# Table rows for the upper partitions from GpSimd's queue, and four wide matmuls in place of 32 narrow ones, in an FFT, soft-MoE and feed-forward kernel

## The chip, the cores and the metric

The kernel runs on one core of a Trainium2 chip. The metric is device time in microseconds of one execution. Three runs of the kernel before took 1397.17, 1400.21 and 1401.28 us: a median of 1400.21, a spread of 4.1 us or 0.3%. One more execution was profiled, and all rows below are from that one.

## The reference

```python
X = np.fft.fft(x, axis=1); X = np.fft.fft(X, axis=2)     # x (8, 3072, 256)
x = X.real.reshape(B * S, D)                             # 24576 tokens of 256
logits = x @ phi                                         # 32 slots
d = softmax(logits, axis=0)                              # over all tokens
slot_input = d.T @ x                                     # 8 experts x 4 slots
slot_out[e] = np.maximum(slot_input[e] @ w1[e], 0) @ w2[e]
c = softmax(logits, axis=1)                              # over the slots
y = c @ slot_out
g = s * np.maximum(y @ w_in, 0) ** 2 + b                 # 256 to 2048
out = g @ w_out                                          # 2048 to 256
```

The transformed tokens are never written out. The logits need only x projected by the transform of phi, transformed along the sequence, and the sums for the slots work likewise on the other side. The sequence of 3072 is split as 24 by 128, so that a transform along it is one matrix product over 128, a set of small tables with the twiddle factors, and one over 24.

## The kernel before, in words

The first 251 us prepare the slots, in stages. Then comes the main loop over blocks of 384 tokens, to the end.

*Pages to T (0 to about 90 us).* The sync queue (SP) loads x in 24 pages of 1 MB (xb). For each of the eight batches `emit_v` projects three pages by phd (tile vt, L394, in two parts per batch), `turn_v` turns the result on TensorE (vq, L415) and copies it to v, and `emit_t` multiplies v by the transform matrix f_sb. The result is T, in PSUM; ScalarE or VectorE copies it to SBUF as tile tt, 32 partitions at a time. The last batch is different. The first half of its T (tpa, L428) is four matmuls of 128 columns, copied by ScalarE in eight copies (L432). The second half (tpb, L439) is 32 matmuls with 32 columns of weights and 64 moving columns; they place their results so that VectorE copies them in two copies (L445).

*Order of the loads.* The sync queue issues in the order of a string, `ORDER`: x pages, four quarters of w_out (raw, "w"), two tables for the logits ("l", ltab, in two pages of 32 positions each), two tables for the sums ("h", htab), and the first pages of x for the sums ("r", xrt). The last x page is followed by one xrt page, the ltab loads (L363), the htab loads (L352) and more xrt pages.

*Tables.* An ltab page has 128 partitions, of which the upper 64 hold the same numbers as the lower 64. Before, the sync queue loads the lower 64 in two transfers of 32 rows, and GpSimd copies them to the upper 64 (L512, L513). An htab page has 112 rows: 0 to 47 and 64 to 111 are the same 48 rows of the table, loaded by two transfers of the sync queue, with zeros from GpSimd between (L350) and in alternate columns (L357).

*Logits (about 90 to 106 us).* 16 groups of eight matmuls (lp, L570) multiply tt by ltab, half of them from partitions 0 to 63 and half from 64 to 127, into six buffers of PSUM. ScalarE copies each group (lg, L583), and VectorE takes its maximum for each slot (cm, L585). After the last one the maximum over all tokens is formed; it is needed before any exponential.

*H, sums, experts, main loop.* H (112 to 145 us): exponentials (dt), 128 matmuls with htab (hp, L652), copies (hh, L643). Sums (145 to 204): products with the second pass over x (racc, L727). Experts (204 to 251). Main loop: y, hidden layer and output for all tokens (L1121, L1151, L1154).

Beside these, VectorE and GpSimd turn w_out from 64-bit to 32-bit floats in the first stage: VectorE's steps on raw and wo (L154 to L174, maximum L222, rests L216), GpSimd's sums into bias (L276), ScalarE's casts (L212).

Instructions on each engine run in the order in which the code is written; a planner's running times (`at`) decide only which engine takes a copy and when the side work on w_out is put in. The change leaves those numbers as they are.

Of the kernel before, what the change touches and what calls it, by code (L numbers as in the profile page):

```python
# [8 lines left out]
F32 = mybir.dt.float32  # L9
# [23 lines left out]
def tile_fft2__then__softmoe__then__act_relu2(  # L33
# [18 lines left out]
    nc = tc.nc  # L52
    P = 128
# [4 lines left out]
    M = 2 * NS1  # L58
# [8 lines left out]
    NR = 32  # L67
# [15 lines left out]
    f_sb = early.tile([P, P], F32, name="f_sb")  # L83
# [259 lines left out]
    tt = tpool.tile([P, 64, NG, NE], F32, name="tt")  # L343
    ltabs, htabs = [], []

    def htab_load(i):

        t, k = page([R, 16, 2, 4 * MH], F32, "htab_t")
        htabs.append((t, k))
        nc.gpsimd.memset(t[32:64], 0.0)  # L350
        for q in range(2):
            nc.sync.dma_start(out=t[64 * q:64 * q + M], in_=htab[:, 32 * i:32 * i + 32].rearrange("r (k q) m -> r k q m", q=2))  # L352
        dma_ready(2.5)

    def htab_clear(i):
# [3 lines left out]
    def ltab_load(i):  # L359
        t, k = page([P, 32, P // 2], F32, "ltab")  # L360
        ltabs.append((t, k))
        for c in range(2):
            nc.sync.dma_start(out=t[NR * c:NR * c + NR], in_=ltab[64 * c:64 * c + M, 32 * i:32 * i + 32].rearrange(  # L363
                "(j g) q m -> g j q m", j=2)[0:NR // 2])
        dma_ready(2.57)

    with tc.tile_pool(name="xtp", bufs=1, side="right") as xtp, tc.tile_pool(name="vp", bufs=1, side="right") as vp, \
            tc.tile_pool(name="ps_v", bufs=1, space=PSUM) as psv:
        mxp[:] = [psv, 4]
        vs = [vp.tile([P, NG, NE, NR], F32, name=f"v{k}") for k in range(2)]  # L370
# [52 lines left out]
        def emit_t(b):  # L423
            bg, bq = divmod(b, NG)
            if b == B - 1:
                t = psv.tile([P, 4, P], F32, tag="vq", name="tpa", bufs=2)
                for k in range(4):
                    nc.tensor.matmul(t[:, k, :], lhsT=vs[bg][:, bq, 4 * k:4 * k + 4, :].rearrange("p j n -> p (j n)"),  # L428
                                     rhs=f_sb, start=True, stop=True)
                for j in range(4):  # L430
                    for c in range(2):
                        nc.scalar.copy(tt[64 * bg + NR * c:64 * bg + NR * c + NR, :, bq, 8 * j:8 * j + 4],  # L432
                                       t[NR * j:NR * j + NR, :, 64 * c:64 * c + 64].rearrange("p e k -> p k e"))
                t = psv.tile([P, 2, 4, 64], F32, tag="vt", name="tpb", bufs=2)
                for k in range(4, 8):
                    for j in range(4):
                        for c in range(2):
                            q = 64 * (j // 2) + NR * c
                            nc.tensor.matmul(t[q:q + NR, j % 2, k - 4, :], lhsT=vs[bg][:, bq, 4 * k + j, :],  # L439
                                             rhs=f_sb[:, 64 * c:64 * c + 64], start=True, stop=True,  # L440
                                             tile_position=(0, q), skip_group_check=True)
                for eh in range(2):
                    src = t[64 * eh:64 * eh + 64].rearrange("p j k m -> p m j k")
                    dst = tt[64 * bg:64 * bg + 64, :, bq, 16 * eh:16 * eh + 16].rearrange("p m (j k) -> p m j k", j=2)
                    nc.vector.tensor_copy(dst[:, :, :, 4:8], src)  # L445
                at["pe"] += 3.0
                return
            t = psv.tile([P, 8, P], F32, tag="tps", name="tps", bufs=2)
            for k in range(8):
                nc.tensor.matmul(t[:, k, :], lhsT=vs[bg][:, bq, 4 * k:4 * k + 4, :].rearrange("p j n -> p (j n)"),  # L450
                                 rhs=f_sb, start=True, stop=True)
            at["pe"] += 2.0
            waiting = any(side_at[w[0]] < at["pe"] + 4 for w in side_work)
            eng = "act" if waiting or b >= B - 4 or at["act"] < at["dve"] + 1 else "dve"
            for j in range(4):
                for c in range(2):
                    busy(eng, 0.7 if eng == "dve" else 0.6)
                    r = 64 * bg + NR * c
                    args = (tt[r:r + NR, :, bq, 8 * j:8 * j + 8],
                            t[NR * j:NR * j + NR, :, 64 * c:64 * c + 64].rearrange("p e k -> p k e"))  # L460
                    if b == B - 2:
                        late_t.append(lambda args=args: nc.scalar.copy(*args))
                    else:
                        (nc.scalar.copy if eng == "act" else nc.vector.tensor_copy)(*args)  # L464
# [44 lines left out]
            f()  # L509
        for n in range(2 * B - 2, 2 * B):  # L510
            turn_v(n)
        nc.gpsimd.tensor_copy(ltabs[0][0][64:P], ltabs[0][0][0:64])  # L512
        nc.gpsimd.tensor_copy(ltabs[1][0][64:P], ltabs[1][0][0:64])  # L513
        for _ in range(4):
            side_step(0.0, True)
        emit_t(B - 1)
# [41 lines left out]
    with tc.tile_pool(name="ps_l", bufs=6, space=PSUM) as psl, \  # L558
# [3 lines left out]
        for st in range(NCH // 2 + SKEW):  # L562
            halves = [(h, st - SKEW * h) for h in range(2) if 0 <= st - SKEW * h < NCH // 2]
            lps = {h: psl.tile([R, KC, NG * NE], F32, name="lp") for h, _ in halves}
            for k in range(2 * KC):
                q = P // 2 * (k % 2)
                m = M if q else P // 2
                for h, i8 in halves:
                    r = slice(64 * h, 64 * h + 64)
                    nc.tensor.matmul(  # L570
                        lps[h][q:q + m, k // 2, :], lhsT=ltabs[i8 // 4][0][r, 2 * KC * (i8 % 4) + k, 0:m],
                        rhs=tt[r, 2 * KC * i8 + k].rearrange("p b e -> p (b e)"), start=True, stop=True,
# [737 lines left out]
```

## Time and profile before

| | |
|---|---|
| three timed runs | 1397.17, 1400.21, 1401.28 us |
| span of the profiled execution | 1411.6 us |
| TensorE matmul passes (PE) | 1388.2 us busy, 98%, x9036 |
| VectorE (DVE) | 1171.9 us busy, 83% |
| ScalarE (ACT) | 1010.7 us busy, 72% |
| GpSimd (POOL) | 233.1 us busy, 17% |
| DMA | 112.27 MB, mean 80 GB/s |

The span is 11.4 us longer than the median of the runs. One fp32 matmul of the code shows as two passes. PE are matmul passes and PEld weight loads; they overlap.

The rows below have these columns. A row of the busy time by stages: the stretch in us, its length, then for PE, PEld, DVE, ACT and POOL the busy time with the number of instructions, then the clock granted to TensorE (1.00 is full speed), the busy share of the 16 DMA engines, and GB/s. A row of a timeline: start and length in us, engine, line, operation, output and inputs, shapes, number of instructions, and in brackets the idle time before it and what ended that. A row of the groups by line: the line, engine, operation, shapes and count, then busy us and mean ns of one, then the idle time just before.

### The profile page before, as it was taken

The numbers are of one execution on the slowest core, as the hardware profiler recorded it, in microseconds if no ns is written. First come the engines' busy times: TensorE is split into PE (matmuls) and PEld (weight loads), VectorE is DVE, ScalarE is ACT, GpSimd is POOL, SyncE is SP. The second block draws the span as 40 slices with busy tenths as digits, with TensorE's granted clock in tenths as the row PEclk, the third lists the DMA queues.
The fourth block names the chain that finished last, engine by engine and source line by source line (L and its number), as shares of the span: only waits on it lengthen the run. The fifth ranks groups of instructions, "written<-read, shape, count | busy, mean of one in ns | idle before, by whom it ended". The sixth has DMA issues, their size and how long they took to land.

```text
span 1411.6 us, 23102 instructions
## 1 busy us (share of the span) xinstructions
PE 1388.2 (98%) x9036; PEld 856.0 (61%) x9036; DVE 1171.9 (83%) x1490; ACT 1010.7 (72%) x1423; POOL 233.1 (17%) x287
## 2 busy tenths in 40 slices
PE   8989999999999999999999999999999999999998
PEld 5669564566666666666666666666666666666665
DVE  1565764998989999999989898989898989888886
ACT  2774314877777777777877787877777777777775
POOL 1143400021212121211112121111111111111110
PEclk9995999999999999999999999999999999999999
DMA  8995795101010101101010101010101010101001
GB/s 352 414 311 229 291 414 225 29 27 36 20 36 23 36 24 29 30 23 32 23 36 21 34 23 36 23 33 23 36 23 36 23 36 23 33 23 36 23 20 30
DMA packets 72381, 112.27 MB, mean 80 GB/s; under 512 B 33904, under 2 KB 59632, under 8 KB 64976
## 3 DMA queue, kind: packets, MB, share of 16 engines
q1 hardware_dynamic: 72144, 110.70, 23.1%
q8 instruction: 71, 1.16, 0.3%
q14 instruction: 38, 0.31, 0.1%
q0 software_dynamic: 128, 0.10, 0.0%
HBM read 78.48 MB, written 25.17 MB: 73 GB/s over the span
## 4 chain that ended last, share of the span: by engine, by line
PE 88%; DMA 2%; DVE 1%; issue 1%; SPq 0%; ACT 0%; POOL 0%; DVEq 0%; ACTq 0%; POOLq 0%
PE op L1151 46%; PE op L1154 23%; PE fhp L1121 12%; PE racc L727 3%; DMA w2t<-in_moe_w_dram 2%; PE hp L652 2%; PE dps L712 1%; PE lp L570 1%; SPq L1084 0%; DVE cm L585 0%; DVE r L1127 0%; DVE rhl L1112 0%; PE eop L957 0%; DMA g<-gs 0%; PE gp L1055 0%
## 5 line engine op out<-in xcount | busy, mean ns | idle before, releaser
L1151 PE MATMUL op<-whl,rhl 128*128 128x512 f16 x3072 | 1025.3, 379 | 0.8 <-ACT rhl L1111 0.6
L1154 PE MATMUL op<-whl,rhl 128*128 128x256 f16 x3072 | 835.7, 273 | 0.0
L1126 ACT ACTIVATE r<-fhp,wsc 128x768 f32<-128x768 f32 (+1 forms) x513 | 461.8, 900 | 230.0 <-PE fhp L1121 228.8
L1127 DVE SCALAR_TENSOR_TENSOR r<-fhp,r 128x768 f32<-128x768 f32 (+1 forms) x513 | 488.9, 953 | 113.6 <-ACT r L1126 104.0
L1112 DVE TENSOR_TENSOR rhl<-r,rhl 128x768 f16<-128x768 f32 x511 | 506.9, 992 | 0.9 <-ACT rhl L1111 0.9
L1151 PEld LDWEIGHTS <-rhl 128*128 128x128 f16 x3072 | 300.5, 98 | 335.4 <-ACT rhl L1111 0.9
L1111 ACT CAST rhl<-r 128x768 f16<-128x768 f32 x511 | 420.1, 822 | 1.8 <-DVE r L1127 1.8
L1154 PEld LDWEIGHTS <-rhl 128*128 128x128 f16 x3072 | 300.6, 98 | 62.7 <-issue 0.3
L1166 POOL TENSOR_TENSOR ot<-ot,bias 128x256 f32<-128x256 f32 x189 | 138.1, 731 | 974.2 <-DVE ot L1164 974.2
L1121 PE MATMUL fhp<-ct,g 128*128 128x384 f16 x1024 | 250.4, 326 | 1.1 <-DMA g<-gs 0.8
L1121 PEld LDWEIGHTS <-g 128*128 128x128 f16 x1024 | 99.9, 98 | 69.0 <-issue 1.1
L1163 ACT ACTIVATE o<-op,small 128x256 f32<-128x256 f32 x189 | 90.0, 477 | 16.7 <-PE op L1154 16.7
L1164 DVE SCALAR_TENSOR_TENSOR ot<-op,small,o 128x256 f32<-128x256 f32 x192 | 91.7, 478 | 0.3
L394 PE MATMUL vt<-xb,phd 128*64 128x384 f32 (+3 forms) x288 | 49.0, 477 | 5.3 <-DMA xb<-in_x_turned_dram 5.3
L727 PE MATMUL racc<-xrt,dh 128*64 128x256 f32 x384 | 44.5, 383 | 0.4 <-DVE dh L717 0.4
L394 PEld LDWEIGHTS vt<-xb,phd 128*64 128x64 f32 x288 | 26.5, 139 | 25.5 <-issue 13.8
L727 PEld LDWEIGHTS racc<-xrt,dh 128*64 128x64 f32 x384 | 26.3, 137 | 20.9 <-issue 4.5
L419 DVE COPY v<-vq 128x512 f32<-128x512 f32 (+1 forms) x15 | 8.3, 593 | 33.9 <-PE vq L415 33.9
L406 ACT COPY vts<-vt 128x512 f32<-128x512 f32 (+1 forms) x16 | 8.5, 533 | 32.1 <-PE vt L394 32.0
L464 ACT COPY tt<-tps 32x512 f32<-32x512 f32 x48 | 27.7, 577 | 4.9 <-PE tps L450 4.4
L652 PE MATMUL hp<-htab_t,dt 112*128 112x104 f32 x128 | 27.6, 422 | 0.2 <-ACT dt L669 0.2
L652 PEld LDWEIGHTS hp<-htab_t,dt 112*128 112x128 f32 x128 | 27.4, 333 | 0.5 <-issue 0.5
(229 smaller groups left out, 518.0 us busy)
## 6 DMA issues: line engine op xcount, KB each, us to landing
xb<-in_x_turned_dram SPq DMA_DIRECT2D x24, 1024.0 KB, 20.1
xrt<-in_x_pages_dram SPq DMA_DIRECT2D x24, 1024.0 KB, 13.9
out_dram<-ot SPq DMA_DIRECT2D x128, 128.0 KB, 1.7
w1t<-in_moe_w_dram SPq DMA_DIRECT2D x8, 1024.0 KB, 13.7
out_dram<-ot SPq DMA_DIRECT2D x128, 64.0 KB, 2.0
raw<-in_moe_w_out_dram SPq DMA_DIRECT2D x4, 1024.0 KB, 20.3
raw<-in_moe_w_in_dram SPq DMA_DIRECT2D x4, 1024.0 KB, 7.8
w2t<-in_moe_w_dram SPq DMA_DIRECT2D x4, 1024.0 KB, 17.8
```

Of the source, the lines that this page charges most:

```text
L652: nc.tensor.matmul(hp[q][:, k, :], start=True, stop=True, lhsT=dt.rearrange("p k g e -> p (k g e)")[:, 128 * (2 * k + q):128 * (2 * k + q) ...
L727: nc.tensor.matmul(raccs[acc][64 * h:64 * h + 64, :], lhsT=dh[:, m, g].rearrange("p j e -> p (j e)"), rhs=xr[k][0][:, g, t, :], start=(sum ...
L1111: nc.scalar.copy(a, r2)
L1112: nc.vector.tensor_tensor(out=l, in0=r2, in1=a, op=ALU.subtract)
L1121: nc.tensor.matmul(hp[k * split][:, k, :].rearrange("p (s b m) -> p s b m", s=2, b=B), lhsT=g16[:, f * P:(f + 1) * P], rhs=c, start=True, ...
L1126: nc.scalar.activation(out=r[:, k], in_=hp[i][:, k], func=AF.Relu, scale=wsc[:, 2, p:p + 1])
L1127: nc.vector.scalar_tensor_tensor(out=r2[:, k], in0=hp[i][:, k], scalar=0.0, in1=r[:, k], op0=ALU.max, op1=ALU.mult)
L1151: nc.tensor.matmul(op.rearrange("p h d -> p (h d)"), lhsT=a, rhs=w.rearrange("p h d -> p (h d)"), start=(f == 0), stop=False)
L1154: nc.tensor.matmul(op[:, 0, :], lhsT=l, rhs=w[:, 0, :], start=False, stop=(f == NFC - 1))
L1163: nc.scalar.activation(out=o1, in_=op[:, 1, :], func=AF.Copy, scale=qv)
L1164: nc.vector.scalar_tensor_tensor(out=ot, in0=op[:, 0, :], scalar=qv, in1=o1, op0=ALU.mult, op1=ALU.add)
L1166: nc.gpsimd.tensor_tensor(out=ot, in0=ot, in1=bias, op=ALU.add)
```

## The change

Tables: `ltab_load` issues four transfers per page in place of two, of 32 rows and 256 KB each. The two for the lower partitions stay on the sync queue, the two for the upper are issued by GpSimd; GpSimd's two copies on the chip go. Of the two htab transfers of a page the one for partitions 64 to 111 moves from the sync queue to GpSimd. T: the second half of the last batch is made like the first half, by four matmuls of 128 columns, and eight copies of 32 partitions on VectorE.

```diff
@@ htab_load @@
         for q in range(2):
-            nc.sync.dma_start(out=t[64 * q:64 * q + M], in_=htab[...])
+            (nc.gpsimd if q else nc.sync).dma_start(out=t[64 * q:64 * q + M], in_=htab[...])
@@ ltab_load @@
         for c in range(2):
-            nc.sync.dma_start(out=t[NR * c:NR * c + NR], in_=ltab[...])
+            for h in range(2):
+                r = 64 * h + NR * c
+                (nc.gpsimd if h else nc.sync).dma_start(out=t[r:r + NR], in_=ltab[...])
@@ emit_t, last batch @@
-                t = psv.tile([P, 2, 4, 64], F32, tag="vt", name="tpb", bufs=2)
+                t = psv.tile([P, 4, P], F32, tag="vt", name="tpb", bufs=2)
                 for k in range(4, 8):
-                    for j in range(4):
-                        for c in range(2):
-                            q = 64 * (j // 2) + NR * c
-                            nc.tensor.matmul(t[q:q + NR, j % 2, k - 4, :], lhsT=vs[bg][:, bq, 4 * k + j, :],
-                                             rhs=f_sb[:, 64 * c:64 * c + 64], start=True, stop=True, ...)
-                for eh in range(2):
-                    src = t[64 * eh:64 * eh + 64].rearrange("p j k m -> p m j k")
-                    dst = tt[64 * bg:64 * bg + 64, :, bq, 16 * eh:16 * eh + 16].rearrange(...)
-                    nc.vector.tensor_copy(dst[:, :, :, 4:8], src)
+                    nc.tensor.matmul(t[:, k - 4, :], lhsT=vs[bg][:, bq, 4 * k:4 * k + 4, :].rearrange("p j n -> p (j n)"),
+                                     rhs=f_sb, start=True, stop=True)
+                for j in range(4):
+                    for c in range(2):
+                        nc.vector.tensor_copy(tt[64 * bg + NR * c:64 * bg + NR * c + NR, :, bq, 8 * j + 4:8 * j + 8],
+                                              t[NR * j:NR * j + NR, :, 64 * c:64 * c + 64].rearrange("p e k -> p k e"))
@@ after turn_v of the last batch @@
-        nc.gpsimd.tensor_copy(ltabs[0][0][64:P], ltabs[0][0][0:64])
-        nc.gpsimd.tensor_copy(ltabs[1][0][64:P], ltabs[1][0][0:64])
```

GpSimd's instructions before, from the memset for the first htab page (htab_t_571) on; bias_76 are the sums of w_out, of which wo_398 is the second half, and ltab_547 and ltab_550 are the two logits tables:

```order
L350 MEMSET htab_t_571 32x1664
L276 TENSOR_TENSOR bias_76<-bias_76,wo_398 128x256 x4
L350 MEMSET htab_t_612 32x1664
L512 COPY ltab_547<-ltab_547 64x2048
L513 COPY ltab_550<-ltab_550 64x2048
L276 TENSOR_TENSOR bias_76<-bias_76,wo_398 128x256 x4
```

The same place now, with the second logits table as ltab_552 and the htab pages as htab_t_575 and htab_t_616:

```order
L365 DMA ltab_547<-in_ltab_dram 32x1x2048 x2
L365 DMA ltab_552<-in_ltab_dram 32x1x2048 x2
L350 MEMSET htab_t_575 32x1664
L352 DMA htab_t_575<-in_htab_dram 48x1664
L276 TENSOR_TENSOR bias_76<-bias_76,wo_398 128x256 x4
L350 MEMSET htab_t_616 32x1664
L352 DMA htab_t_616<-in_htab_dram 48x1664
L276 TENSOR_TENSOR bias_76<-bias_76,wo_398 128x256 x4
```

The four ltab transfers stand ahead of the first memset, where GpSimd had nothing; the second htab transfer stands behind the first sums of wo_398; the two copies behind the second memset are gone.

TensorE's instructions before, from the end of the last batch's projection (vt) over its turning (vq) and T (tpa, tpb) to the first logits (lp); v_113 is the second half of the v tiles:

```order
L394 MATMUL vt<-xb,phd 64x256
L394 MATMUL vt<-xb,phd 64x128
L415 MATMUL vq<-ident,vts 128x128 x7
L428 MATMUL tpa<-f_sb,v_113 128x128 x4
L439 MATMUL tpb<-f_sb,v_113 32x64 x32
L190 MATMUL warm<-ones 128x128 x4
L570 MATMUL lp<-tt,ltab 64x128
```

The same place now:

```order
L396 MATMUL vt<-xb,phd 64x256
L396 MATMUL vt<-xb,phd 64x128
L417 MATMUL vq<-ident,vts 128x128 x7
L430 MATMUL tpa<-f_sb,v_113 128x128 x4
L438 MATMUL tpb<-f_sb,v_113 128x128 x4
L190 MATMUL warm<-ones 128x128 x4
L566 MATMUL lp<-tt,ltab 64x128
```

Nothing is reordered: 32 narrow matmuls have become four wide ones, 28 fewer, between the first half of T and the four matmuls on ones that precede the logits.

VectorE's instructions before, from the last steps on w_out's fourth quarter (wo, wsc) to the maxima of the logits:

```order
L174 SCALAR_TENSOR_TENSOR wo<-raw,wo 128x1024
L222 TENSOR_REDUCE wsc<-wo 128x2
L204 TENSOR_SCALAR wsc<-wsc 128x2
L205 RECIPROCAL wsc<-wsc 128x2
L445 COPY tt<-tpb 64x64x2x4 x2
L585 TENSOR_REDUCE cm<-lp 112x32 x13
```

And now:

```order
L174 SCALAR_TENSOR_TENSOR wo<-raw,wo 128x1024
L222 TENSOR_REDUCE wsc<-wo 128x2
L204 TENSOR_SCALAR wsc<-wsc 128x2
L205 RECIPROCAL wsc<-wsc 128x2
L442 COPY tt<-tpb 32x64x4 x8
L581 TENSOR_REDUCE cm<-lp 112x32 x13
```

The copies stand where they stood, eight of 32 partitions in place of two of 64.

## Rows read from the trace of the kernel before

**Rows 1.** Busy time by stages: the H stage and the main loop

```profile
112.00:145.00 33.00, 32.78 (x151) 31.66 (x151) 14.27 (x26) 16.44 (x34) 12.19 (x10) 0.51 0.46 182
...
251.00:1411.00 1160.00, 1156.18 (x7113) 695.92 (x7113) 1038.38 (x1276) 902.39 (x1224) 179.46 (x223) 1.00 0.11 29
```

**Rows 2.** Sync queue's timeline and its transfers: the last x page

```profile
60.43 1.73 SPq L289 DMA_DIRECT2D xb<-in_x_turned_dram  x1
...
xb<-in_x_turned_dram SPq DMA_DIRECT2D x1, 1024.0 KB, 20.5
```

**Rows 3.** TensorE's timeline, 66 to 84 us: parts of the projection

```profile
68.07 4.97 PE L394 MATMUL vt<-xb,phd 128*64 128x384 f32 x32 [0.42 <-DMA xb<-in_x_turned_dram]
...
81.28 2.38 PE L394 MATMUL vt<-xb,phd 128*64 128x384 f32 x20
```

**Rows 4.** VectorE's timeline, 84 to 104 us

```profile
88.19 1.39 DVE L445 COPY tt<-tpb 64x512 f32<-64x512 f32 x2
92.20 4.50 DVE L585 TENSOR_REDUCE cm<-lp 112x32 f32<-112x512 f32 x7 [2.61 <-ACT lg L583]
100.98 1.29 DVE L585 TENSOR_REDUCE cm<-lp 112x32 f32<-112x512 f32 x2 [4.28 <-ACT lg L583]
102.69 1.29 DVE L585 TENSOR_REDUCE cm<-lp 112x32 f32<-112x512 f32 x2 [0.42 <-ACT lg L583]
```

**Rows 5.** Chain that ended last, 84 to 112 us: start, us, what

```profile
95.01 3.88 issue
98.89 4.80 PE lp L570 x86
```

**Rows 6.** DMA queues: whole span, 78.6 to 96.3, 96.3 to 97.6 us

```profile
q8 instruction: 71, 1.16, 0.3%
...
q14 instruction: 1, 0.01, 0.1%
...
q8 instruction: 1, 0.02, 5.6%
```

**Rows 7.** Busy time in 78.6 to 95.1 us

```profile
78.60:95.10 16.50, 14.08 (x251) 11.01 (x248) 11.34 (x17) 14.98 (x31) 4.76 (x4) 1.00 1.03 214
```

**Rows 8.** GpSimd's timeline, 50 to 96 us

```profile
54.90 3.15 POOL L276 TENSOR_TENSOR bias<-bias,wo 128x256 f32<-128x256 f32 x4 [15.45 <-DVE wo L174]
63.59 1.48 POOL L350 MEMSET htab_t<- 32x1664 f32 x1 [5.54 <-PE vt L394]
...
89.32 1.89 POOL L512 COPY ltab<-ltab 64x2048 f32<-64x2048 f32 x1 [12.06 <-DMA ltab<-in_ltab_dram]
```

**Rows 9.** Busy time while x alone moves, and while the tables move

```profile
20.00:58.00 38.00, 36.99 (x258) 24.91 (x254) 19.03 (x27) 21.60 (x40) 5.05 (x7) 1.00 1.02 415
86.00:92.00 6.00, 4.48 (x123) 4.08 (x125) 3.44 (x6) 5.83 (x14) 1.89 (x1) 1.00 1.03 183
```

**Rows 10.** TensorE's timeline, 84 to 104 us: the matmuls before the pause

```profile
94.36 0.65 PE L570 MATMUL lp<-tt,ltab 64*64 64x128 f32 x10 [0.17 <-DVE cm L585]
```

**Rows 11.** Groups by line and shape, 86 to 90 us

```profile
L439 PE MATMUL tpb<-f_sb,v 128*32 128x64 f32 x64 | 1.1, 221 | 0.0
```

**Rows 12.** Groups by line and shape, VectorE, 145 to 205 us

```profile
L717 DVE COPY dh<-dps 128x256 f32<-128x256 f32 x2 | 0.8, 424 | 0.6 <-PE dps L712 0.6
```

**Rows 13.** ScalarE's timeline, 84 to 104 us

```profile
87.22 2.98 ACT L432 COPY tt<-tpa 32x256 f32<-32x256 f32 x8
90.22 1.33 ACT L212 ACTIVATE whl<-wo,wsc 128x512 f16<-128x512 f32 x2
```

**Rows 14.** Groups by line and shape, 112 to 145 us

```profile
L652 PE MATMUL hp<-htab_t,dt 112*128 112x104 f32 x128 | 27.6, 422 | 0.2 <-ACT dt L669 0.2
...
L669 ACT ACTIVATE dt<-dt 112x512 f32<-112x512 f32 x15 | 9.3, 627 | 0.4 <-POOL dt L633 0.4
...
L643 ACT COPY hh<-hp 128x208 f32<-128x208 f32 x16 | 8.2, 514 | 13.5 <-PE hp L652 13.5
```

More of the change, by code (lines that the diff above doesn't have):

```diff
@@ L351, in htab_load @@
         for q in range(2):
-            nc.sync.dma_start(out=t[64 * q:64 * q + M], in_=htab[:, 32 * i:32 * i + 32].rearrange("r (k q) m -> r k q m", q=2))
+            (nc.gpsimd if q else nc.sync).dma_start(out=t[64 * q:64 * q + M], in_=htab[:, 32 * i:32 * i + 32].rearrange("r (k q) m -> r k q m", q=2))
         dma_ready(2.5)
@@ L362, in ltab_load @@
         for c in range(2):
-            nc.sync.dma_start(out=t[NR * c:NR * c + NR], in_=ltab[64 * c:64 * c + M, 32 * i:32 * i + 32].rearrange(
-                "(j g) q m -> g j q m", j=2)[0:NR // 2])
+            for h in range(2):
+                r = 64 * h + NR * c
+                (nc.gpsimd if h else nc.sync).dma_start(
+                    out=t[r:r + NR], in_=ltab[64 * c:64 * c + M, 32 * i:32 * i + 32].rearrange("(j g) q m -> g j q m", j=2)[0:NR // 2])
         dma_ready(2.57)
@@ L433, in emit_t @@
                                        t[NR * j:NR * j + NR, :, 64 * c:64 * c + 64].rearrange("p e k -> p k e"))
-                t = psv.tile([P, 2, 4, 64], F32, tag="vt", name="tpb", bufs=2)
+                t = psv.tile([P, 4, P], F32, tag="vt", name="tpb", bufs=2)
                 for k in range(4, 8):
-                    for j in range(4):
-                        for c in range(2):
-                            q = 64 * (j // 2) + NR * c
-                            nc.tensor.matmul(t[q:q + NR, j % 2, k - 4, :], lhsT=vs[bg][:, bq, 4 * k + j, :],
-                                             rhs=f_sb[:, 64 * c:64 * c + 64], start=True, stop=True,
-                                             tile_position=(0, q), skip_group_check=True)
-                for eh in range(2):
-                    src = t[64 * eh:64 * eh + 64].rearrange("p j k m -> p m j k")
-                    dst = tt[64 * bg:64 * bg + 64, :, bq, 16 * eh:16 * eh + 16].rearrange("p m (j k) -> p m j k", j=2)
-                    nc.vector.tensor_copy(dst[:, :, :, 4:8], src)
+                    nc.tensor.matmul(t[:, k - 4, :], lhsT=vs[bg][:, bq, 4 * k:4 * k + 4, :].rearrange("p j n -> p (j n)"),
[4 more added lines that the diff above has]
+                                              t[NR * j:NR * j + NR, :, 64 * c:64 * c + 64].rearrange("p e k -> p k e"))
                 at["pe"] += 3.0
```

## The prediction

> **What bounds the kernel now.** I read the busy time by stages first, then the chain of waits, then the rows of the stretch that the change touches. The last 1,160 us (from 251 to 1411) are TensorE at its full clock, busy for 1156.2 of them [rows 1]; nothing in the change reaches that loop. What the change touches lies between 58 and 112 us, and from there on every stage waits for the one before: the pages for the sums (145 to 204) come free as TensorE uses them. So a microsecond won or lost before 112 us comes out at the end as about one microsecond, and I cost only that stretch.
>
> The stretch has two bounds in turn. Up to 83 us it is the stream of x pages. The sync queue keeps its transfers about 20 us ahead: the last x page was issued at 60.43 and landed 20.5 us later, at 80.9 [rows 2]; TensorE began the work that needs it at 81.28, one stage earlier it stood 0.42 us for a page, and otherwise it runs without a gap [rows 3]. Transfers and TensorE are level, with 0.4 us to spare: whatever holds the last pages up holds TensorE up.
>
> From 90 us it is the logits stage: TensorE fills PSUM (L570), ScalarE copies, VectorE takes the maxima, about 0.64 us each (seven in 4.50) [rows 4]. Its chain has one odd piece: from 95.01 TensorE stands 3.88 us with "issue", waiting for nothing that the profile shows, and then runs 4.80 us [rows 5]. VectorE finishes its backlog and then idles 4.28 us; with the short wait behind it (0.42) and another like it some 5.0 us go [rows 4]. I read this as TensorE waiting for its own instructions. Its 18,072 matmul passes and weight loads (9036 each) come in 71 packets of the instruction queue q8 [rows 6], about 255 to a packet. Between 78.6 and 95.1 TensorE uses 251 + 248 = 499 of them [rows 7], two packets' worth, and up to 96.3 no q8 packet lands (the one instruction packet of that time is q14's); the next of q8 falls into 96.3 to 97.6 [rows 6], and TensorE goes on 1.3 us later. The DMA engines are full then, with the tables.
>
> **The change, part by part.**
>
> Upper table rows from GpSimd's queue. Four transfers of 256 KB (1.05 MB) are new: the upper halves of ltab were copied on chip before. Two of 312 KB move from the sync queue. The order shows where: GpSimd issues the ltab rows before its first memset for htab. In the trace GpSimd is done with its sums at 54.90 + 3.15 = 58.05 and stands 5.54 us idle until that memset [rows 8]; the new issues wait for data long landed and for a VectorE step near 60 us, so they leave at 58 to 61 us. That is beside the x pages still in flight, not behind them as the sync queue's own ltab rows are. htab's first 0.32 MB follows the memset, still ahead of the last x pages; its second comes after VectorE's work on w_out, too late to hold x up.
>
> What 1.37 MB cost the x stream has two bounds. At the rate of loads into all 128 partitions, 415 GB/s [rows 9], 3.3 us. At the rate when the tables alone are moving, into 32 or 48 partitions, 183 GB/s [rows 9], 7.5 us. I take the value nearer to the second: all the new rows go into the upper 64 partitions, so I give them half of 415, 207 GB/s, while the other half goes on with x: 6.6 us. Less the 0.4 us to spare: +6.2 us on the start of everything after x. The floor below would be 0, if GpSimd's transfers only used gaps; the DMA share over 20 to 58 us is 1.02 [rows 9], so there are none, but I keep it as a rival.
>
> [...]
>
> What goes: GpSimd's two copies, the first from 89.32 on, 1.89 us [rows 8], the second as long behind it. From its start to the pause TensorE stood 0.17 us, and for VectorE [rows 10]; worth 0.
>
> T's last half. TensorE: 64 passes of 0.22 us in 1.1 us go [rows 11], eight like those of the first half in about the same time come; worth 0. VectorE: two copies of 64x512 in 1.39 us [rows 4] become eight of 32x256. A copy of 128x256 out of PSUM takes 0.424 us [rows 12]; eight make 3.39. From the same start (88.19) they end at 91.58 and not 89.58. ScalarE's own eight copies end at 87.22 + 2.98 = 90.20 [rows 13], which was what the logits stage waited for; now it waits for VectorE, 1.38 us more. But ScalarE casts weights until 90.22 + 1.33 = 91.55 before its first copy of logits [rows 13]. The matmuls ahead of the pause, about one group of logits, take 0.65 us [rows 10]: begun at 91.58 they are done at 92.23, so that copy starts 0.65 us later and no more: +0.65 us. Bounds 0.2 (0.36 us a copy, as on ScalarE) and 1.4. Queued behind the eight copies on VectorE is only the first maximum, which waits for that same copy.
>
> The pause. The order shows 28 fewer matmuls just before the logits, each two passes and two weight loads: 112 instructions fewer. So the packet that TensorE lacked is needed 28 matmuls later in the logits, at the 90th instead of the 62nd of 128. By then VectorE has about five groups of logits in hand, some 3 us of cover (5 x 0.64). But the packet is also asked for later, inside the logits. With the fetch taking as long behind x and table traffic as it does now, I get a pause of about 3 us of which 1 shows: 4 of the 5.0 us come back. Two bounds: all 5.0 come back, or none, if the fetch falls worse.
>
> Here the profiled execution has to be set against the timed runs. Its span is 1411.6 us, the median of the runs 1400.2, 11.4 us less. The last 1,160 us have no such slack, so the timed runs are shorter in the first 251 us, and the pause may be one of the things that they don't have; then nothing comes back. I take half of the 4 us: -2.0.
>
> Sum: +6.2 + 0.65 - 2.0 = +4.85 us. Against the profiled span that is 1416.4; against the median of the runs 1405.0, which I predict.
>
> **Rivals.**
>
> 1. The x stream is held up by the smaller bound alone (3.3 - 0.4 = 2.9): 2.9 + 0.65 - 2.0 = +1.55, 1401.8. For it: 16 engines share the packets. Against: the table rows of [rows 9] at half the rate.
> 2. x is late by the full 6.2, but the pause is in the timed runs and goes whole: 6.2 + 0.65 - 5.0 = +1.85, 1402.1. For it: three runs within 4 us of each other, so the pause is there always or never.
> 3. Faster: GpSimd's transfers don't hold up x, as a queue whose packets are served after the sync queue's, and the pause goes: 0.65 - 5.0 = -4.35, 1395.9. It decides where x is late by less than 0.15 us (0.15 + 0.65 - 5.0 = -4.2). Against: no gap in the DMA share before 80 us.
> [...]
> 5. The pause stays as long as it is or grows, with the x delay of the larger bound (7.1): 7.1 + 0.65 = +7.75, 1408.0.
>
> [...]
>
> **How the numbers follow.** My forecast 0.42, rival 1 0.22, rival 2 0.13, rival 3 0.10, rival 4 0.04, rival 5 0.09. A measurement of this kernel can tell from no change about 0.3%, 4.2 us: slower is above 1404.4, faster below 1396.0. Slower: 0.42 + 0.09 = 0.51. Rivals 1 and 2 are no change, 0.35, with 0.01 of rival 3's near edge 0.36. Faster: 0.10 + 0.04 less that edge, 0.13. The range holds forecast, rivals 1 and 2, and rival 5 with the larger bound (7.1 + 1.4 + 0.5 = 9.0, 1409.2), and reaches towards rival 3 without all of it: 1396.5 to 1409.5. The forecast's own range is 1403 to 1408.
>
> **What would show it.** The x step: the last three x pages land 3 to 7 us later than 20 us after their issue and TensorE stands as long for them before the last quarter of v; wrong, if they land as before. The copies: VectorE's eight end after ScalarE's eight, and the first logits matmul waits for VectorE. The pause: a stretch of "issue" on TensorE inside the logits, at about the 90th matmul, with VectorE idle about 1 us; if it is as long as before and VectorE idle 4 us, the term is wrong. The copies on GpSimd are gone and nothing has moved for them. The whole is wrong if the logits stage begins no later than now, or if the time changes behind 251 us.

## The result, and the profile after

The changed kernel takes 1411.77 us (median of 4 runs, 1410.15 to 1414.52) where the kernel before took 1400.74 (4 runs): a ratio of 1.0089, 95% interval 1.0074 to 1.0104. It is slower by about 11 us. The forecast was +4.85, with a range that ended at 1409.5: the sign was right, the size less than half.

The span of its profiled execution is 1412.7 us, 1.1 more than that of before. That comparison misleads, and the first experiment shows why: in some executions of several of these kernels TensorE runs the H stage at a lower granted clock (0.50 for its matmuls in before, 1.00 in the changed kernel), they take 27.6 us and not 14.5, and the whole takes some 13 us more, as in the profiled executions of before, ltab_only and late_rows and, by their times, in 3 of the 86 timed runs of before and in 4 of the 12 of t_only, the most of any kernel beside late_rows (2 of 6).

TensorE's timeline of the changed kernel (start, us, engine, line, operation, shapes, count; in brackets the idle time before it and what ended that), against [rows 3]:

```profile
78.11 7.39 PE L396 MATMUL vt<-xb,phd 128*64 128x384 f32 x32 [9.95 <-DMA xb<-in_x_turned_dram]
...
95.95 3.84 PE L396 MATMUL vt<-xb,phd 128*64 128x384 f32 x20 [2.15 <-DMA xb<-in_x_turned_dram]
...
108.43 11.73 PE L566 MATMUL lp<-tt,ltab 64*64 64x128 f32 x256 [3.75 <-ACT whl L212]
```

TensorE stands for x twice, 12.1 us in all, where it stood 0.42. The sync queue's timeline and its transfers say the same of the last x page, against [rows 2]:

```profile
60.85 5.53 SPq L289 DMA_DIRECT2D xb<-in_x_turned_dram  x1
...
xb<-in_x_turned_dram SPq DMA_DIRECT2D x1, 1024.0 KB, 35.0
```

It was issued at nearly the same time as before (60.85 us, then 60.43), and took 35.0 us in place of 20.5. The chain that ended last (start, us, what) has it as one piece:

```profile
60.85 34.97 DMA xb<-in_x_turned_dram
```

GpSimd's timeline shows what was put beside it, against [rows 8]:

```profile
56.12 3.14 POOL L276 TENSOR_TENSOR bias<-bias,wo 128x256 f32<-128x256 f32 x4 [14.68 <-DVE wo L174]
59.20 1.03 POOL L365 DMA_DIRECT2D ltab<-in_ltab_dram  x2
61.46 0.98 POOL L365 DMA_DIRECT2D ltab<-in_ltab_dram  x2 [1.23 <-DVE whl L216]
64.05 1.48 POOL L350 MEMSET htab_t<- 32x1664 f32 x1 [1.62 <-PE vt L396]
65.48 0.50 POOL L352 DMA_DIRECT2D htab_t<-in_htab_dram  x1
```

The busy time by stretches (the last three numbers: TensorE's clock, the busy share of the DMA engines, GB/s), against [rows 9]:

```profile
20.00:58.00 38.00, 38.00 (x263) 26.88 (x260) 18.91 (x26) 20.91 (x38) 3.89 (x6) 0.98 1.02 415
63.00:77.00 14.00, 5.16 (x39) 3.57 (x35) 5.66 (x7) 6.49 (x12) 1.93 (x2) 0.85 1.03 237
87.00:91.00 4.00, 4.00 (x27) 2.56 (x26) 2.95 (x5) 3.74 (x7) 0.00 (x0) 1.00 1.04 250
```

While GpSimd's rows are in flight (63 to 77, and 87 to 91 for the second htab page) the DMA engines are as busy as before, but x and tables together move at 237 and 250 GB/s, not at 415.

After each stand TensorE's matmuls are slower: the 32 passes at 78.11 take 7.39 us where they took 4.97, and the 20 at 95.95 take 3.84 where they took 2.38 [rows 3]. The clock granted from 95.95 to 99.73 us was 0.60 on average, 1.00 at first and 0.50 from 96.75 us on:

```profile
95.95:99.73 3.78, 3.77 (x21) 2.40 (x21) 0.00 (x0) 0.00 (x0) 0.00 (x0) 0.60 1.07 171
```

The copies of T and what follows, VectorE's timeline first, then ScalarE's, against [rows 4, 13]:

```profile
104.75 3.47 DVE L442 COPY tt<-tpb 32x256 f32<-32x256 f32 x8
```

```profile
103.35 2.98 ACT L434 COPY tt<-tpa 32x256 f32<-32x256 f32 x8
106.35 1.33 ACT L212 ACTIVATE whl<-wo,wsc 128x512 f16<-128x512 f32 x2
110.47 0.58 ACT L579 COPY lg<-lp 112x512 f32<-112x512 f32 x1 [2.78 <-PE lp L566]
```

VectorE's eight copies take 3.47 us and end at 108.22, 1.9 us after ScalarE's (106.33), and TensorE's logits begin at 108.43: it waits for VectorE, though the row names a cast of ScalarE that had been done for 0.7 us. (In wide_t below, which has the same copies, the row of the same wait names VectorE's.) The logits then run 11.73 us without a pause.

### The profile page after: what moved, and what is told of

Same layout as the page of the kernel before. It is cut to its first block, busy times and chain, and to the rows that moved or that the text cites. A ratio compares the mean times of both kernels' runs of the same rounds, so it can differ in the third digit from the quotient of the medians.

```text
span 1412.7 us, 23014 instructions
## 1 busy us (share of the span) xinstructions
PE 1377.3 (97%) x8980; PEld 844.6 (60%) x8980; DVE 1173.5 (83%) x1496; ACT 1009.2 (71%) x1423; POOL 232.1 (16%) x291
## 4 chain that ended last, share of the span: by engine, by line
PE 91%; DMA 6%; DVE 2%; SPq 1%; ACT 1%; issue 0%; DVEq 0%; ACTq 0%
PE op L1147 46%; PE op L1150 23%; PE fhp L1117 12%; DMA xb<-in_x_turned_dram 3%; PE racc L723 3%; PE vt L396 3%; DMA w2t<-in_moe_w_dram 2%; PE hp L648 1%; PE dps L708 1%; DVE cm L581 1%; PE tps L448 1%; SPq L1080 0%; PE lp L566 0%; PE vq L417 0%; DVE r L1123 0%
## 5 line engine op out<-in xcount | busy, mean ns | idle before, releaser
L396 PE MATMUL vt<-xb,phd 128*64 128x512 f32 (+3 forms) x288 | 54.0, 519 | 16.0 <-DMA xb<-in_x_turned_dram 16.0
L396 PEld LDWEIGHTS vt<-xb,phd 128*64 128x64 f32 x288 | 30.7, 151 | 36.4 <-issue 19.6
L462 ACT COPY tt<-tps 32x512 f32<-32x512 f32 x48 | 27.6, 576 | 5.1 <-PE tps L448 4.6
L770 POOL TENSOR_TENSOR lg<-lg,rm 112x512 f32<-112x512 f32 x16 | 22.4, 1404 | 4.2 <-DVE rm L768 4.2
L752 POOL TENSOR_TENSOR lg<-et,lg 112x512 f16<-112x512 f32 x16 | 18.5, 1156 | 0.0
## 6 DMA issues: line engine op xcount, KB each, us to landing
w1t<-in_moe_w_dram SPq DMA_DIRECT2D x8, 1024.0 KB, 13.3
```

The source lines that it names most:

```text
L396: nc.tensor.matmul(vt[64 * h:64 * h + 64, o:o + k, :], lhsT=phd[:, c, sg, :], rhs=turned(pg, c, i, k, rev), start=(c == 0 and m < 2), stop ...
```

## Experiments

Each of these kernels was timed against the kernel before, 6 or 12 times; only b_again, extra_upper and extra_even were run once, for their profiles. Diffs are against the kernel before. In the expectations "theory A" and "theory B" are two explanations that the run is to tell apart.

**b_again: the kernel before, once more.** No edit.

> The kernel before, unchanged, profiled once more. In its first profile the 128 hp matmuls of the H stage took 27.61 us at half clock and the span was 1411.6 us, 11 us above the timed runs; in the profile of the changed kernel they took 14.51 at full clock. Theory A (the half clock of that stage belonged to that one profiled execution): hp takes about 14.5 us here, the span is about 1411.6 - 13.1 = 1398.5, and the pause on TensorE in the logits is there or not independently of it. Theory B (the half clock is part of every execution of the kernel before, and the profiler costs 11 us elsewhere): hp takes 27.6 us again, span 1411 to 1412.

Measured: span 1399.4 us. The groups by line of before ([rows 14]: 27.6 us) have here

```profile
L652 PE MATMUL hp<-htab_t,dt 112*128 112x104 f32 x128 | 14.6, 276 | 0.2 <-DMA xrt<-in_x_pages_dram 0.2
```

and TensorE's timeline has the pause, in two parts (the last part of x, the first logits, the pause, and the beginning of H):

```profile
82.60 2.37 PE L394 MATMUL vt<-xb,phd 128*64 128x384 f32 x20 [0.66 <-DMA xb<-in_x_turned_dram]
...
91.57 6.20 PE L570 MATMUL lp<-tt,ltab 64*64 64x128 f32 x124 [1.52 <-ACT tt L432]
100.21 2.64 PE L570 MATMUL lp<-tt,ltab 64*48 64x128 f32 x86 [2.44 <-issue]
...
106.50 0.69 PE L570 MATMUL lp<-tt,ltab 64*64 64x128 f32 x4 [1.74 <-issue]
...
114.67 14.57 PE L652 MATMUL hp<-htab_t,dt 112*128 112x104 f32 x128 [0.21 <-DMA xrt<-in_x_pages_dram]
```

Theory A. The 11.4 us between the profiled span and the runs were the H stage at the lower clock, 27.6 - 14.6 = 13.0 us (granted 0.50 from 114.5 to 142.2 us of before, 0.98 from 112 to 146 us here); the pause is in this undisturbed execution too. From here on b_again stands for the profile of before.

**t_only and tables_only: one part of the change each.**

```diff
 t_only:      32 narrow matmuls and two copies -> four wide ones and eight copies; tables as before
 tables_only: ltab_load, htab_load as in the change, GpSimd's copies gone; T as before
```

> The kernel before with the T part of the change alone: four matmuls of 128 columns, eight copies on VectorE; tables as before. Theory A (the table rows on GpSimd's queue are the whole loss): x lands as before (last page at about 80.9 us), VectorE's eight copies take 3.4 us and end 1.4 to 2 us later than the two did, the pause is shorter by 1 us or more; time within 2 us of before, 1399 to 1403. Theory B (the copies and the later start of the logits carry a good part of the loss): 1404 to 1408.

> The kernel before with the tables part of the change alone: upper ltab rows and second htab rows from GpSimd's queue; T by 32 matmuls and two copies as before. Theory A (the table rows are the whole loss, because x packets slow down beside them): last x page lands at about 95.8 us and not 80.9, TensorE stands about 9.5 us for a page and then about 2 us for the last; time 1409 to 1413. Theory B (about half of the loss is T's): 1404 to 1408.

Measured: t_only 1402.2 us, ratio 1.0036 (1.0006 to 1.0065), or 1400.0 against 1399.98 without its four longer executions (1413.6 to 1418.4). tables_only 1410.8 us, ratio 1.0086 (1.0069 to 1.0102), nearly the whole change. Theory A for both: the loss is the tables', unless T makes the longer executions more frequent, which these runs don't decide (wide_t below, with the same T, has 2 in 12, wide_tables none). In t_only TensorE's timeline shows both sides of T:

```profile
96.86 10.68 PE L566 MATMUL lp<-tt,ltab 64*64 64x128 f32 x256 [3.51 <-ACT whl L212]
```

It stands 3.51 us before the logits (1.52 in b_again), and then no pause stops it. Against theory A, x did not land as before in this execution: TensorE stood 3.16 us for the last page, with nothing new beside x. Of tables_only, TensorE's wait for the page was

```profile
77.71 7.96 PE L396 MATMUL vt<-xb,phd 128*64 128x384 f32 x32 [9.76 <-DMA xb<-in_x_turned_dram]
```

The second wait of theory A, about 2 us for the last page, is not there: that page landed at 93.1 us, not at 95.8, in an execution that was the shortest of its six (1407.3 us).

**ltab_only: the upper ltab rows alone from GpSimd.**

```diff
+            for h in range(2):
+                r = 64 * h + NR * c
+                (nc.gpsimd if h else nc.sync).dma_start(out=t[r:r + NR], in_=ltab[...])
-        nc.gpsimd.tensor_copy(...)   # both copies
```

> The kernel before with the upper ltab rows alone from GpSimd's queue as in the change (four transfers of 32 rows, 1.05 MB, at 58 to 62 us), no copies; htab on the sync queue, T as before. Theory A (the loss goes with the narrow rows in flight beside x): the x page that TensorE needs at about 68 us is late by 7 to 8 us and not 10; all of x is late by that; time +6 to +9, 1405 to 1408. Theory B (the htab rows carry the loss, being the ones still in flight when the last x pages are): +1 to +3.

Measured: 1406.85 us, ratio 1.0052 (1.0022 to 1.0083); TensorE stood 8.13 us for the page. Theory A: ltab has 7.5 us of the loss. That leaves some 3 to 4 us of tables_only's for the htab rows, by difference: they were not run alone.

**wide_extra, wide_gp, gp64: is it the queue, the bytes, or how the rows lie?**

```diff
 wide_extra: + nc.gpsimd.dma_start(out=junk, in_=xt[0] as 128 rows of 7 KB)      # 0.92 MB, nothing reads it
 wide_gp:    ltab stored as two pages of 128 rows;  nc.gpsimd.dma_start(out=t, in_=ltab[i])   # 2.1 MB
 gp64:       same storage; + nc.gpsimd.dma_start(out=t[64:128], in_=ltab[i, 64:128])          # 1.05 MB
```

> The kernel before, with one extra transfer that nothing reads: 0.92 MB of x into all 128 partitions (128 rows of 7 KB), issued by GpSimd where the change issues the upper ltab rows (at about 58 us). Theory A (the loss comes from rows that go into few partitions: such a packet takes 0.5 to 0.6 us and makes the x packets beside it take as long, 0.56 to 0.63 us against 0.315): here packets stay at about 0.3 us, x is late by 0.92 MB at 415 GB/s = 2.2 us, TensorE stands 1.5 to 2.5 us more for pages, time +1 to +3, 1401 to 1403. Theory B (GpSimd's queue beside the sync queue is what slows x, whatever it writes): x late by 5 us or more, time +5 to +9, 1405 to 1409.

> ltab stored in the order of the 128 partitions and loaded whole by GpSimd's queue in two transfers of 1 MB at the change's place (58 to 62 us); the sync queue loads no ltab; no copies; htab and T as before. Twice the bytes beside x that the change's ltab rows have, but wide. Theory A (narrowness): packets at 0.31 to 0.32 us, x late by 2.1 MB at 415 GB/s = 5 us, and the tables are there before x, so the logits wait for nothing; time +3 to +5. Theory B (bytes or queue decide): x late by 12 us or more, time +9 or more.

> As the run with the upper ltab rows alone, same queue, same time of issue, same bytes, but ltab is stored in the order of the partitions and the upper 64 rows of a page go in one transfer of 64 partitions in place of two of 32. The lower rows are loaded by the sync queue in two transfers of 32 rows as before. Theory A (what slows packets is how few partitions are being written at a time): packets beside x take clearly less than 0.55 us, x is late by 3 to 5 us, time +2 to +5. Theory B (it is the upper partitions, or the second queue, or the bytes): as the other run, +6 to +9.

Measured: wide_extra 1402.55 us, ratio 1.0034 (1.0014 to 1.0055), 3.4 us more than before, just above theory A's range; wide_gp 1402.15, ratio 1.0010 (0.9987 to 1.0033), less than theory A's +3 to +5; gp64 1407.71, ratio 1.0051 (1.0020 to 1.0083). For x TensorE stood 2.65 us in wide_extra, 5.46 in wide_gp and 8.17 in gp64 (8.13 in ltab_only). The busy time of 63 to 69 us, one row each of ltab_only, gp64, wide_gp and wide_extra:

```profile
63.00:69.00 6.00, 5.43 (x42) 3.77 (x38) 1.09 (x2) 4.09 (x8) 1.48 (x1) 1.00 1.06 224
```

```profile
63.00:69.00 6.00, 4.10 (x32) 2.81 (x28) 1.09 (x2) 4.11 (x8) 1.48 (x1) 1.00 1.04 259
```

```profile
63.00:69.00 6.00, 4.18 (x30) 2.77 (x27) 1.09 (x2) 3.96 (x8) 1.48 (x1) 1.00 1.02 415
```

```profile
63.00:69.00 6.00, 6.00 (x48) 4.44 (x44) 1.05 (x2) 3.76 (x8) 1.48 (x1) 1.00 1.02 418
```

The same queue, the same time: 415 and 418 GB/s with rows for all 128 partitions, 224 and 259 with rows for the upper 64 alone. Twice the bytes, wide, cost less than the narrow ones. So it is neither the second queue nor the bytes. gp64 went against theory A: 64 rows in one transfer are as slow as 32. That left open whether the number of rows counts or where they go.

**extra_upper and extra_even: 64 rows, two places.**

```diff
 extra_upper: + nc.gpsimd.dma_start(out=junk[64:128],  in_=xt[0] rows 0 to 63 of 7 KB)
 extra_even:  + nc.gpsimd.dma_start(out=junk[0:128:2], in_=xt[0] rows 0 to 63 of 7 KB)
```

> The kernel before, with one extra transfer that nothing reads: 64 rows of 7 KB (0.46 MB) of x into partitions 64 to 127, from GpSimd's queue where the change issues the upper ltab rows. Into all 128 partitions such rows took 0.276 us each. Theory A (what slows packets is that the rows of one transfer go into neighbouring partitions of one half): packets here take 0.45 to 0.6 us, the x packets beside them 0.55 us or more. Theory B (it is something about the ltab rows, their source or their size): 0.28 us as in the wide transfer.

> The same extra transfer, the same 64 rows of 7 KB at the same place, but into the 64 even partitions, so that it spreads over the whole width. Theory A (the place of the rows decides, not their number): packets take about 0.28 us and x's beside them 0.315, as in the wide transfer. Theory C (64 rows are too few whatever partitions they go to): packets as in the run with the upper 64.

Measured, busy time of 62 to 64 us, extra_upper and extra_even:

```profile
62.00:64.00 2.00, 2.00 (x18) 1.39 (x14) 0.00 (x0) 1.22 (x3) 0.67 (x1) 1.00 1.02 196
```

```profile
62.00:64.00 2.00, 2.00 (x21) 1.34 (x17) 0.00 (x0) 0.80 (x2) 0.11 (x1) 1.00 1.04 409
```

With the same 64 rows everything together moves at 196 GB/s when they go into the upper half and at 409 when they are spread over the even partitions. Where the rows go decides, not how many there are (theory A). One part of the expectation was missed: the sync queue's big rows beside extra_upper's averaged 397 ns and not 550 or more. Only 15 began in that time, most of them towards its end; of the 2 KB rows that moved before them, the 47 that began in 62 to 64 us took 187 ns, against 87 in extra_even. How late x was tells little here, with 0.46 MB and one execution each: TensorE stood 3.15 us for the page in the one and 2.57 in the other, where x was late before the extra rows came. From the DMA records of the traces, GpSimd's rows and the sync queue's rows of 6.5 to 8 KB in flight beside them, number and mean time of one:

```
                       GpSimd's rows        sync queue's rows beside
changed kernel, 63-77  176 x 511 ns         198 x 591 ns
changed kernel, 87-90   48 x 444 ns          60 x 588 ns
ltab_only              128 x 586 ns         190 x 543 ns
gp64                   128 x 573 ns          84 x 526 ns
wide_gp                256 x 320 ns          91 x 315 ns
wide_extra             128 x 276 ns         130 x 316 ns
extra_upper             64 x 498 ns          15 x 397 ns
extra_even              64 x 279 ns          36 x 321 ns
```

**early_sp, tables_sp, late_rows: the same rows at other places.**

```diff
 early_sp:  -ORDER = "xxxwxxxxxxwxxxxxxwxxxxwxrllhhrr"
            +ORDER = "xxxwxxxxxxwxxxxxxwllxxxxwxrhhrr"
 tables_sp: upper ltab rows loaded as in the change, but all by nc.sync; GpSimd's copies gone
 late_rows: in the place of GpSimd's copies: a one-column copy, then nc.gpsimd.dma_start of the upper rows
```

> The kernel before with its four ltab transfers (1.05 MB, lower 64 partitions, 32 rows each) moved forward on the sync queue, ahead of the last five x pages and the last quarter of w_out; copies on GpSimd and T as before. Theory A (narrow rows are slow wherever they are, and interleaved with x they cost more): the rows in one queue, one behind the other, take about the 5.7 us that they took before, so TensorE stands 4.5 to 6 us for x; behind x only htab is left, so the logits start with tables long there; time +2 to +5, 1402 to 1405. Theory B (narrow rows cost x nothing as long as they are in the sync queue): no wait for x, time -2 to +1.

> The kernel before with the upper ltab rows loaded too, but by the sync queue, behind the lower rows of each page and so behind x; no copies on GpSimd; htab on the sync queue, T as before. The bytes are those of the change. Theory A (place and queue decide, not the bytes): x lands as before; the second ltab page is complete 5 to 6 us later than before (about 97 to 99 us), which the logits stage meets after its first eight groups; the first page is complete 2.5 to 3 us later: time +2 to +5, 1402 to 1405. Theory B (the bytes into the upper partitions cost the same wherever they are): +9 to +11, 1409 to 1411.

> The kernel before with the upper ltab rows from GpSimd's queue as in the change, but issued only when the lower rows of the same page have landed (a one-column copy from the lower into the upper half, in the place of the two full copies, is what they wait for); htab and T as before. Theory A (the loss is that the rows are issued beside x pages that TensorE is about to need): x lands as before, last at about 80.9; the upper rows land some 5 to 7 us after the copies would have been done, the logits stage starts or stalls that much later, less the pause that it hides: time +2 to +6, 1403 to 1407. Theory B (GpSimd's queue is slow by itself: 1.37 MB took about 17 us in the changed kernel, 59.2 to 77.9): the upper rows land more than 12 us after their issue and the time is 1409 or more.

Measured: early_sp 1411.06 us, ratio 1.0088 (1.0068 to 1.0107). tables_sp 1400.8, ratio 1.0018 (1.0002 to 1.0033). late_rows 1412.3, ratio 1.0112 (1.0076 to 1.0148), its four shorter runs 1408.75 to 1412.44. TensorE's timeline of early_sp, then of tables_sp:

```profile
78.67 7.42 PE L394 MATMUL vt<-xb,phd 128*64 128x384 f32 x32 [10.44 <-DMA xb<-in_x_turned_dram]
```

```profile
68.09 4.97 PE L396 MATMUL vt<-xb,phd 128*64 128x384 f32 x32 [0.45 <-DMA xb<-in_x_turned_dram]
83.84 2.37 PE L396 MATMUL vt<-xb,phd 128*64 128x384 f32 x20 [2.47 <-DMA xb<-in_x_turned_dram]
```

With all 2.1 MB of ltab behind x, the change's bytes cost about 2 us: the place decides. early_sp refutes both theories in their sizes. Only the lower rows, in one queue, no GpSimd, and the wait for the page is about as long as the change's first one (9.95 us): 10.44 us for 1.05 MB and not 5.7. That narrow rows on some engines are in flight beside x rows on others is inferred from the times: x rows and ltab rows have the same 8 KB, and all 171 rows of that size that began between 63 and 71 us took long, 0.67 us on average and none less than 0.59.

late_rows went against theory A: x was not held up as in the change (2.49 us for its last page), but TensorE, which began the logits at 94.11, then stood for the upper rows themselves (its timeline):

```profile
105.73 7.20 PE L573 MATMUL lp<-tt,ltab 64*64 64x128 f32 x160 [10.31 <-DMA ltab<-in_ltab_dram]
```

GpSimd issued them from 92.76 on, the first row moved at 98.36, 5.6 us later (3.8 in the changed kernel), and then they shared the engines with the second pass over x, at 0.58 us a row. Theory B has the size; that the queue is slow by itself is not shown, since wide_gp's two transfers, of twice the bytes, were done 8.4 and 9.9 us after their issue.

**wide_tables and wide_t: can the experiments' version beat both?**

```diff
+        nc.sync.dma_start(out=t.rearrange("p q m -> p (q m)"), in_=ltab[i])   # 128 rows of 8 KB, for both
-        for c in range(2): nc.sync.dma_start(...)                            # the narrow loads
-        nc.gpsimd.tensor_copy(...)                                           # both copies
 wide_t: also four wide matmuls and eight copies, as in the change
```

> The kernel before with ltab stored in the order of the 128 partitions (the same numbers, the upper half repeated) and loaded by the sync queue in two transfers of 1 MB into all 128 partitions, in the place of the four narrow ones; no copies on GpSimd; htab and T as before. Theory A (narrow rows are what is slow: 183 GB/s against 415): 2.1 MB take 5.05 us where 1.05 MB took about 5.7, and no copy follows; the second page is there 1 to 3 us sooner than its copy was; time -3 to +1, 1397 to 1401. Theory B (what counts is bytes): 2.1 MB take twice the time of the narrow rows, the logits start 3 to 5 us later, 1403 to 1405.

> A version that could beat both: ltab in two wide transfers on the sync queue behind x, no copies on GpSimd, and the T part of the change (four matmuls, eight copies on VectorE). The wide tables alone gave a ratio of 0.9997 to before, T alone 1.0036. Theory A (T's 28 matmuls fewer shorten the pause on TensorE, its copies cost 1 to 2 us): 1398 to 1402, not different from before by more than 0.3%. Theory B (with the tables early, the shorter pause comes out at the end): 1393 to 1396.

Measured: wide_tables 1398.62 us, ratio 0.9997 (0.9984 to 1.0011); wide_t 1399.54 us, ratio 1.0000 (0.9967 to 1.0034). Both are well ahead of the changed kernel and not apart from before. The tables were hardly what the logits waited for: in b_again TensorE's weight loads stood 0.5 us for GpSimd's copy, in the first profile of before not at all. wide_t's logits run without a pause and take 11.67 us, from their first matmul to the matmuls on ones behind them, against 14.00 in wide_tables; they begin 8.58 us after TensorE starts its last turning (vq), against 6.65. T gives back 2.3 us in the pause and takes 1.9 in the copies.

## Why the prediction was right in sign and wrong in size

*What bounds the kernel.* Right: x and TensorE were level, and what held x up held TensorE up. The 0.4 us to spare were not there in every execution: for the last page TensorE stood 0.66 us in b_again, 2.47 in tables_sp and 3.16 in t_only, with nothing from GpSimd beside x. So a difference of 2 or 3 us in x's arrival between two single profiles shows nothing here.

*Where the new transfers go.* Right for the ltab rows and the first htab rows: GpSimd issued them at 59 to 66 us, beside the x pages in flight, htab's behind its memset. Wrong for the second htab transfer, which the prediction had as too late to hold x up: x itself was late by then, and 48 rows at 87 to 90.5 us fell on its last pages.

*The price of 1.37 MB: the step that failed.* The prediction gave the new rows half of the engines' rate "while the other half goes on with x", 6.6 us: an estimate, which no run shows. Its bounds came from stretches with only wide rows or nearly only narrow ones. Beside each other, the narrow rows take 0.51 us, and x's rows take 0.59 us in place of 0.315: the x stream pays for the narrow rows and a second time for its own. From the records of the changed kernel, over 16 engines: the narrow rows (with the second htab transfer, 1.69 MB) 176 x 0.511 / 16 + 48 x 0.444 / 16 = 6.95 us; and the time that the sync queue's rows took above 0.314 us (the big ones) and 0.086 (those of 2 KB) in the same two stretches is 5.0 us. Together that is 12.0 us of the engines' time. TensorE began its last part of x at 95.95 us in place of 82.60 in b_again: the x term is +13.4, of which these two bills explain 12.0, and not +6.2. Rival 5's 7.1 was too low as well. The trace of before had a stretch with rows of both kinds in flight, which the prediction didn't use. From 92.1 us on, with the ltab rows landed, the last htab rows move beside the first xrt pages, which fill all 128 partitions: up to 96 us 31 htab rows took 549 ns each and 69 xrt rows 633 ns, and all together moved at about 200 GB/s.

```profile
92.00:96.00 4.00, 2.84 (x90) 2.36 (x80) 3.68 (x6) 3.19 (x7) 3.70 (x4) 1.00 1.01 202
```

The prediction's larger bound, 7.5 us at 183 GB/s, leaves out the second half of the bill too. Rows into 64 neighbouring partitions in one transfer cost as much as rows into 32 in each of two (gp64 beside ltab_only, 1.0051 and 1.0052). Two wide transfers moved at 415 GB/s together with x (wide_gp), and extra_even adds that 64 rows are enough for such a rate, 409 GB/s, if they are spread over the whole width.

*The clock behind the stand.* The prediction had no term for it. In the changed kernel the last part of x, begun after a stand of 2.15 us, ran at a granted clock of 0.60 and took 1.5 us longer than in b_again (3.84 us, then 2.37; in the profile of before 2.38, at 1.00). A stand does not always do this: in t_only the same part took 2.37 us after a stand of 3.16.

*The copies.* Priced at 3.39 us, measured 3.47; VectorE ends 1.9 us after ScalarE (forecast 1.38). But the term was +0.65, because ScalarE's cast was to cover the rest, and that failed. Counted from TensorE's last turning, the logits begin 2.0 us later than in b_again in the changed kernel and 1.6 in t_only, and ScalarE's first copy of logits then waits for TensorE and not for the cast: 2.78 us in the changed kernel, where the clock granted from 108.43 to 110.47 us was 0.50, and 1.48 us in t_only, where the copy starts 1.16 us after the first logits and not 2.04 (ScalarE's timeline):

```profile
98.02 0.59 ACT L579 COPY lg<-lp 112x512 f32<-112x512 f32 x1 [1.48 <-PE lp L566]
```

In t_only that copy starts 1.5 us later than in b_again, counted in the same way: as much as the forecast's upper bound of 1.4.

*The pause.* Half of 4 us was to come back. Against b_again the logits are 3.9 us shorter in the changed kernel, and no pause is left, neither at the 90th matmul nor elsewhere. It is gone in all three profiles with 112 instructions fewer ahead of the logits (t_only, wide_t, the changed kernel). With the old T ten profiles have a pause of 1 us or more, but early_sp and extra_even don't (0.26 and 0.69 us), so the number of instructions is not all. The records of the instruction queue q8 bear the reading out: in each of these ten TensorE went on 1.2 to 1.4 us after a packet had landed, and that packet landed 4.8 to 7.4 us after the first logits had begun; in early_sp and extra_even it landed 3.3 and 2.5 us after. No run varied the fetch alone. The pause is in an undisturbed execution, so rival 2 had that half right; it did not come out at the end as 5 us, since T's copies take back 1.9 of the 2.3 us that it gives (wide_t against wide_tables).

*The profiled span against the runs.* The prediction had the pause as what the timed runs might lack. It was the clock of the H stage, 13.0 us, which the sum didn't touch. No run shows rival 4, to which the chances give 0.04 as faster: the matmuls of H took 14.5 us in the changed kernel and 14.6 in b_again, so nothing was won there.

*Sum.* The forecast's terms as TensorE's rows have them, the changed kernel against b_again: x +13.4 (forecast +6.2), the clock behind the stand +1.5 (none), the copies +2.0 (+0.65), the logits without the pause -3.9 (-2.0), from there to H +0.1. That gives +13.1, and the matmuls of H begin at 127.79 us in place of 114.67:

```profile
127.79 14.51 PE L648 MATMUL hp<-htab_t,dt 112*128 112x104 f32 x128 [0.22 <-ACT dt L665]
```

The two spans are 13.3 us apart (1412.7 and 1399.4). The medians of the runs are 11.0 apart: the profiled execution of the changed kernel was the longest of its four. So three of the forecast's terms were off and one was missing. All but the x term come to -0.3 together, by luck of their signs: the loss is the x term.

## What to carry to other kernels

Price a transfer that is put beside another one by what both then take, and take the rate from a stretch in which rows of both kinds are in flight: here rows into half of the partitions nearly doubled the time of full-width rows beside them (0.59 us, not 0.315), and a stretch of that kind stood in the trace of before. Count also what the matmuls behind a longer stand may take: here 32 passes took 7.39 us behind 9.95 us, at a clock of 0.67 on average, in place of 4.97 at 1.00. Where a stream of loads is level with the engine that uses it, put everything else behind it (tables_sp 1400.8 us, early_sp 1411.06), or lay the rows out so that each transfer is spread over all 128 partitions (wide_gp 1402.15, gp64 1407.71). And before a sum is set against a profiled span that is 11 us off the timed runs, look for a stage of that profile at a lower clock, as H was here at 0.50.

## What the runs showed of the hardware

- 64 rows of 7 KB into partitions 64 to 127 took 498 ns each beside x, the same 64 rows into the even partitions 279 ns.
- The sync queue's full-width rows of 8 KB took 526 to 591 ns beside GpSimd's narrow rows in the changed kernel, ltab_only and gp64, and 315 beside its wide ones in wide_gp. In early_sp, with one queue, the 171 rows of 8 KB that began between 63 and 71 us took 0.67 us on average.
- From GpSimd's issue of a transfer to its first row: 3.8 us in the changed kernel, 5.6 us in late_rows.
- In ten traces TensorE's "issue" pause inside the logits ended 1.2 to 1.4 us after a packet of the instruction queue q8 had landed; the pause lasted 1.03 us in gp64 and 3.88 in the profile of before.
- After a stand of 9.95 us the next 32 passes took 7.39 us, at a granted clock of 0.50 from 78 to 82 us; after a stand of 0.42 us they took 4.97, at 1.00.
- The H stage's 128 matmuls took 27.6 us in three profiled executions (before, ltab_only, late_rows) and 14.5 to 14.7 in the other thirteen. Shortly ahead of them TensorE stood 1.25 and 0.97 us in the profile of before, with the matmuls of H behind it at 0.50, and 1.67 and 0.97 us in the changed kernel, with H at 1.00. What decides between the two clocks was not tested.
